# Moving w_down in 4-KB pieces and shifting two zero fills behind the first block's w_down stores

## The chip, the cores, the metric

One core of one Trainium2 chip. The metric is device time in microseconds (us), the median of several executions. All runs quoted here were in the fast state. "Ratio" is the mean time of one kernel's fast runs over that of the other's in the same rounds, so not quite the ratio of the medians that stand beside it. Profile times are counted from the start of the span, which is some 2 us shorter than the measured time.

## The reference

Forward and backward pass of one adaLN-conditioned block: attention of one query token over the last 4096 cached positions, then a gated feed-forward part. Every gradient is an output, so those of the K and V caches are written in full (65,536 positions, zeros outside the window). Only the feed-forward part is touched:

```python
g = jnp.einsum('bsd,df->bsf', x, w_gate)        # D = 1024, F = 3584
u = jnp.einsum('bsd,df->bsf', x, w_up)
h = _sigmoid(g) * u
return jnp.einsum('bsf,fd->bsd', h, w_down)     # w_down is [3584, 1024] bf16
```

## The kernel before

The program moves 248 MB, about half of it zeros (126 MB; "fills", 1 MB each, read from a tile of zeros and issued by GpSimd between other transfers, so that the DMA engines never idle). The feed-forward part runs in 7 blocks of 512 columns. Each block loads w_up and w_gate (GpSimd) and w_down in two halves of 512 KB (SyncE), computes, overwrites the weights in place with their gradients, and stores these (GpSimd). The w_down tile has one buffer, so a block's load waits until the block before has stored the same half.

```python
Z_FOLD = (3, 4)                         # fills at two places ahead of block 0
...
wd_v = ar(152, 8).rearrange("p (i d) -> p i d", i=4)

def wd_dram(t, q, s):                   # half s of block q: rows p and p + 128 on partition p
    return t[q * FB + s * 256:q * FB + s * 256 + 256, :].rearrange("(j p) d -> p j d", p=P)

def load_wd(q, s):
    nc.sync.dma_start(out=wd_v[:, 2 * s:2 * s + 2, :], in_=wd_dram(B_w_down, q, s))

def store_wd(q, s):
    nc.gpsimd.dma_start(out=wd_dram(out_8, q, s), in_=wd_v[:, 2 * s:2 * s + 2, :])
...
load_ug(1, 0, 4); load_ug(1, 4, 4)      # (on two lines in the kernel)
zero(Z_FOLD[1])                         # 4 fills, in GpSimd's order ahead of block 0's stores
...
front(0); gates(0); hh_ops(0)
ffn_mm(0, 0); wd_ttr(0, 0); wd_outer(0, 0)   # wd_outer: VectorE product, then store_wd
ffn_mm(0, 1); wd_ttr(0, 1); dug_part(0); wd_outer(0, 1)
load_wd(1, 0); load_wd(1, 1)
for q in range(NB):
    ...                                 # 8 x (VectorE reduce, ScalarE product), stores of block q
    front(q + 1); gates(q + 1); side(); hh_ops(q + 1)
    ffn_mm(q + 1, 0); wd_ttr(q + 1, 0)
    if q + 2 < NB: load_ug(q + 2, 0, 4)
    wd_outer(q + 1, 0)                  # GpSimd, in order, waits here for VectorE
    ...
```

## Time and profile before

| | before |
|---|---|
| time, median of the first 3 runs | 607.25 us |
| bytes moved, mean rate | 248.19 MB, 410 GB/s |
| 2048-byte packets on the hardware queue | 7680, of which 3584 are w_down loads |

The DMA engines are the bound: they are busy for nine tenths or more of every slice of the span but the first and the last, and no compute engine is. So two numbers matter: how much engine time a byte costs, and how long the engines have too little to move. The prediction shows the lines.

### The profile page before, as it was taken

How to read it: one execution, taken by the hardware profiler on the slowest of the kernel's cores; microseconds unless marked ns; L12 is line 12 of the kernel's file. 1: busy time of each engine (PE TensorE's matmuls, PEld its weight loads, DVE VectorE, ACT ScalarE, POOL GpSimd, SP SyncE). 2: the span in 40 equal slices, each digit the busy share in tenths (PEclk: the TensorE clock that was granted, in tenths of full speed). 3: DMA queues.
4: the chain of work that ended last, by engine and by line, in shares of the span. 5: the costliest groups of instructions: out<-in, count | busy, mean ns of one | idle time of the engine just before them, and what ended most of it. 6: DMA issues, size and time to landing. Idle time of an engine off the chain costs nothing.

```text
span 605.6 us, 10906 instructions
## 1 busy us (share of the span) xinstructions
PE 388.1 (64%) x4496; PEld 265.6 (44%) x4516; DVE 325.1 (54%) x616; ACT 282.4 (47%) x426; POOL 177.8 (29%) x281
## 2 busy tenths in 40 slices
PE   3997788999899989989450454344343277757200
PEld 3995434334344446648340353333333256656200
DVE  3754498999511010060462866756667288778420
ACT  3489514557211014228181768558385833764100
POOL 0002121221322212313342464364542523132230
PEclk9999699999999989989755555555555585755555
DMA  8999999999999999999999999999999999999997
GB/s 353 419 417 421 409 426 413 413 419 420 420 425 426 424 426 419 402 425 411 403 412 391 374 396 409 407 416 404 409 414 420 420 423 411 421 424 425 426 416 282
DMA packets 49522, 248.19 MB, mean 410 GB/s; under 512 B 5629, under 2 KB 5629, under 8 KB 29056
## 3 DMA queue, kind: packets, MB, share of 16 engines
q0 software_dynamic: 37792, 210.78, 90.4%
q1 hardware_dynamic: 11632, 36.71, 17.6%
q8 instruction: 35, 0.57, 0.4%
q14 instruction: 15, 0.12, 0.1%
q10 hardware_dynamic: 48, 0.01, 0.0%
HBM read 61.87 MB, written 185.60 MB: 409 GB/s over the span
## 4 chain that ended last, share of the span: by engine, by line
PE 35%; DMA 29%; DVE 17%; ACT 8%; issue 7%; POOL 1%; ACTq 0%; POOLq 0%; another core or an unknown queue 0%; DVEq 0%; SPq 0%
DMA out_dram<-arena 15%; PE b_ps L687 14%; DMA arena<-in_B_w_down_dram 9%; PE n_ps L635 6%; DVE arena L206 4%; DVE arena L193 4%; DMA arena<-in_B_w_gate_dram 3%; DVE arena L210 3%; DVE junk L210 3%; ACT arena L241 2%; PE t_ps L597 2%; DMA arena<-in_B_w_up_dram 2%; PE tp_wq L453 2%; PE w_ps L394 2%; PE tp_k L434 1%
## 5 line engine op out<-in xcount | busy, mean ns | idle before, releaser
L169 POOL DMA_DIRECT2D out_dram<-zeros x112 | 61.6, 550 | 203.8 <-PE q_ps L471 50.4
L687 PE MATMUL b_ps<-arena 128*128 128x512 bf16 x372 | 88.2, 389 | 0.6
L836 PE MATMUL tp_side<-ident_bf,arena 128*128 128x128 bf16 x416 | 50.1, 297 | 50.9 <-ACT arena L837 41.9
L837 ACT COPY arena<-tp_side 128x1024 bf16<-128x1024 bf16 x52 | 52.1, 1010 | 56.6 <-PE tp_side L836 56.4
L193 DVE TENSOR_TENSOR arena<-arena 128x2048 bf16<-128x2048 bf16 x64 | 76.5, 1224 | 2.3 <-PE n_ps L635 0.3
L210 DVE CUSTOM_DVE_ANT_0 arena<-arena,scr 128x1024 bf16<-128x1024 bf16 x56 | 65.2, 1222 | 9.4 <-ACT scr L969 9.4
L635 PE MATMUL n_ps<-arena 128*128 128x512 bf16 x248 | 65.0, 378 | 7.0 <-DVE arena L193 5.1
L836 PEld LDWEIGHTS <-arena 128*128 128x128 bf16 x416 | 41.1, 137 | 56.2 <-issue 56.1
L241 ACT ACTIVATE arena<-scr,h 128x1024 bf16<-128x1024 bf16 x56 | 61.0, 1145 | 0.0
L687 PEld LDWEIGHTS <-arena 128*128 128x128 bf16 x384 | 37.7, 100 | 46.5 <-issue 7.1
L210 DVE CUSTOM_DVE_ANT_0 junk<-arena,b1k 128x1024 bf16<-128x1024 bf16 x28 | 34.3, 1224 | 26.9 <-DMA arena<-in_B_w_down_dram 26.4
L873 POOL DMA_DIRECT2D out_dram<-arena x42 | 30.7, 734 | 45.8 <-ACT arena L241 38.1
L635 PEld LDWEIGHTS <-arena 128*128 128x128 bf16 x256 | 24.6, 97 | 41.8 <-issue 16.4
L1134 ACT ACTIVATE arena<-ps_kv 128x512 bf16<-128x512 f32 x48 | 26.2, 687 | 28.4 <-PE ps_kv L1130 28.2
L599 ACT CAST arena<-t_ps 128x512 bf16<-128x512 f32 x56 | 30.1, 589 | 12.1 <-PE t_ps L597 12.1
L1130 PE MATMUL ps_kv<-junk,arena 8*128 8x128 bf16 x256 | 26.9, 303 | 11.6 <-DVE arena L206 10.3
L949 PE MATMUL fg<-hh_bf,arena 128*128 128x1 bf16 x224 | 8.1, 166 | 40.5 <-DMA arena<-in_B_w_down_dram 38.8
L1130 PEld LDWEIGHTS <-arena 8*128 8x128 bf16 x256 | 25.0, 140 | 13.3 <-issue 13.3
L202 DVE CAST arena<-b_ps 128x512 bf16<-128x512 f32 x5 | 3.5, 692 | 47.1 <-PE b_ps L687 47.1
L949 PEld LDWEIGHTS <-arena 128*128 128x128 bf16 x224 | 7.1, 105 | 43.5 <-DMA arena<-in_B_w_down_dram 41.4
L455 ACT COPY arena<-tp_wq 128x1024 bf16<-128x1024 bf16 x23 | 21.8, 1032 | 8.1 <-PE tp_wq L453 8.1
L206 DVE TENSOR_SCALAR arena<-arena,cs_col 128x4096 bf16<-128x4096 bf16 (+1 forms) x16 | 16.0, 1017 | 8.2 <-DMA out_dram<-arena 8.0
(297 smaller groups left out, 650.7 us busy)
## 6 DMA issues: line engine op xcount, KB each, us to landing
out_dram<-zeros POOLq DMA_DIRECT2D x112, 1024.0 KB, 13.8
out_dram<-arena POOLq DMA_DIRECT2D x32, 1024.0 KB, 18.9
out_dram<-arena POOLq DMA_DIRECT2D x36, 512.0 KB, 9.3
arena<-in_A_wq_dram SPq DMA_DIRECT2D x8, 1024.0 KB, 19.9
out_dram<-zeros POOLq DMA_DIRECT2D x8, 960.0 KB, 12.7
arena<-in_B_w_down_dram SPq DMA_DIRECT2D x14, 512.0 KB, 10.6
out_dram<-arena POOLq DMA_DIRECT2D x28, 256.0 KB, 10.3
arena<-in_A_wo_dram SPq DMA_DIRECT2D x6, 1024.0 KB, 25.0
```

The source lines that it names most:

```text
L169: ins = nc.gpsimd.dma_start(out=region.bitcast(FP32), in_=zeros[:, :])
L193: return nc.vector.tensor_tensor(out=out, in0=a, in1=b, op=op)
L206: return nc.vector.tensor_scalar(out=out, in0=a, scalar1=s1, scalar2=None, op0=op0)
L210: return nc.vector.tensor_tensor_reduce(out=out, in0=w, in1=b, scale=1.0, scalar=0.0, op0=ALU.mult, op1=ALU.add, accum_out=acc)
L241: return nc.scalar.activation(out=out, in_=b, func=ACT.Copy, scale=col)
L599: nc.scalar.copy(out=o, in_=ps)
L635: mm = nc.tensor.matmul(nbank[k][:, :], lhsT=k_nat[:, g, t_ * DH:(t_ + 1) * DH], rhs=vp[:, t_ % 2, 4 * k:4 * k + 4, :].rearrange("p h d -> ...
L687: mm = nc.tensor.matmul(bbank[p][k][:, :], lhsT=a4[:, p, h, :], rhs=wo_t[u][:, a, k * 512:(k + 1) * 512], start=(i == 0 and a == 0), stop= ...
L836: nc.tensor.transpose(tp[:, i * P:(i + 1) * P], blk[:, i * P:(i + 1) * P], ident_bf[:, :])
L837: nc.scalar.copy(out=blk, in_=tp[:, :])
L873: nc.gpsimd.dma_start(out=ug_part(view, q, j0, n), in_=ug_tile(q, k, j0, n))
L1130: nc.tensor.matmul(ps[:, t4 * DH:(t4 + 1) * DH], lhsT=rows[32 * g:32 * g + HG, t_ * P:(t_ + 1) * P], rhs=hd[32 * g:32 * g + HG, :], start= ...
```

## The change

The intent: larger pieces (two neighbouring rows of 2 KB each on one partition are 4 KB of consecutive memory) and an earlier reload of w_down. As a partition now holds rows 2p and 2p+1, the weights of the gate matmuls are taken with a step of 2, and ScalarE's copy of the gradients' row restores the order.

```diff
-Z_FOLD = (3, 4)
+Z_FOLD = (3, 2, 2)
@@ wd_dram
-        return t[q * FB + s * 256:q * FB + s * 256 + 256, :].rearrange("(j p) d -> p j d", p=P)
+        return t[q * FB + s * 256:q * FB + s * 256 + 256, :].rearrange("(p j) d -> p j d", j=2)
@@ front
+                f0 = 256 * (i // 2) + i % 2
-                    ... lhsT=ug_v[:, q % 2, j // 4, j % 4, k, i * P:(i + 1) * P],
+                    ... lhsT=ug_v[:, q % 2, j // 4, j % 4, k, f0:f0 + 255:2],
@@ dug_part
-        nc.scalar.copy(out=dug_b, in_=tp[:, :])
+        nc.scalar.copy(out=dug_b.rearrange("p (s f j) -> p s f j", s=4, j=2),
+                       in_=tp.rearrange("p (s j f) -> p s f j", s=4, j=2))
@@ after block 0's stores
     wd_outer(0, 1)
+    zero(Z_FOLD[2])
     load_wd(1, 0)
```

## The prediction

> **What bounds the kernel now.** I read the head of the page and its slices first, then the page's chain of waits, then rates by stretch, then the chain in order of time, then GpSimd's own timeline.
>
> ```profile
> span 605.6 us, 10906 instructions
> ...
> DMA  8999999999999999999999999999999999999997
> ...
> DMA packets 49522, 248.19 MB, mean 410 GB/s; under 512 B 5629, under 2 KB 5629, under 8 KB 29056
> ...
> PE 35%; DMA 29%; DVE 17%; ACT 8%; issue 7%; POOL 1%; ACTq 0%; POOLq 0%; another core or an unknown queue 0%; DVEq 0%; SPq 0%
> ```
>
> The DMA engines are at 9 or more tenths in every slice but the first and the last, while no compute engine is (PE 64%, DVE 54%). 248.19 MB at 410 GB/s is 605 us: the span. The chain names PE first, but chain shares only say who was waited for; the bytes set the end. So this change, which moves the same bytes, can gain in two ways only: a better rate while bytes flow, or less time in which they don't. The stage it touches is the feed-forward part, about 280 to 480 us.
>
> ```profile
> 320.00:330.00 10.00, 0.14 (x5) 0.14 (x6) 0.16 (x1) 0.00 (x0) 2.29 (x4) 0.50 1.09 410
> 330.00:335.00 5.00, 2.67 (x48) 2.26 (x46) 4.43 (x9) 1.01 (x1) 1.57 (x3) 0.50 0.67 251
> 335.00:340.00 5.00, 2.17 (x18) 1.72 (x17) 3.61 (x10) 2.40 (x3) 3.65 (x6) 0.50 1.06 398
> 340.00:350.00 10.00, 4.33 (x79) 4.00 (x79) 7.88 (x14) 9.95 (x11) 3.27 (x6) 0.50 1.07 394
> ```
>
> The columns are the stretch, its length, busy time of PE, PEld, DVE, ACT and POOL with instructions, then the TensorE clock, the DMA share and GB/s. There is one hole: 251 GB/s at 330 to 335 us. The next stretches come back to 390 to 420, and nowhere later until the tail does the DMA share fall under 1.
>
> ```profile
> 306.13 13.08 DMA out_dram<-arena
> 319.21 0.02 SPq L856
> 319.24 0.04 issue
> 319.27 10.54 DMA arena<-in_B_w_down_dram
> 329.82 0.02 issue
> 329.84 1.22 DVE junk L210
> ...
> 333.43 0.71 POOL out_dram L859
> ```
>
> This is the chain (start, length, what) through the hole. The store of block 0's first w_down half takes 13.08 us to land, because it queues behind what GpSimd issued before. Only then may the load of block 1's half go into the same buffer; it takes 10.54 us. VectorE then works, and GpSimd can issue the next store at 333.43.
>
> ```profile
> 304.42 0.56 POOL L169 DMA_DIRECT2D out_dram<-zeros  x1 [0.58 <-DMA arena<-in_B_w_up_dram]
> 306.13 0.72 POOL L859 DMA_DIRECT2D out_dram<-arena  x1 [1.15 <-DMA arena<-in_B_w_gate_dram]
> 307.50 0.73 POOL L859 DMA_DIRECT2D out_dram<-arena  x1 [0.64 <-ACT arena L837]
> 312.52 1.51 POOL L873 DMA_DIRECT2D out_dram<-arena  x2 [4.30 <-ACT arena L241]
> ...
> 323.63 0.76 POOL L869 DMA_DIRECT2D arena<-in_B_w_gate_dram  x1 [0.55 <-DMA out_dram<-arena]
> 333.43 0.71 POOL L859 DMA_DIRECT2D out_dram<-arena  x1 [9.04 <-DVE arena L206]
> ```
>
> GpSimd issues in order. From 324.4 to 333.4 us it stands still for 9.04 us waiting for that product, and what it queued before runs dry at about 333: the hole. It also stands idle 4.30 us before 312.52, right after the two stores.
>
> **What the Trainium skill says.** (1) "DMA: Bandwidth & Descriptors", Why small descriptors are slow (HBM only): each packet has a fixed cost of some 3 cycles inside the engine. The trace agrees and gives the size. In its packet records (each packet's queue, bytes and time), SyncE's 2048-byte packets take 84 ns where little else interferes (505 to 545 us on the records' own clock, which runs some 7 us ahead of the span's), 4096-byte ones 159 ns and 8192-byte ones 309 ns: 9 ns plus 75 ns per 2 KB. (2) The same page, Queues, rings and completion order: an engine switches between queue rows at packets. That fits 2048-byte packets that took 126 ns while the other queue was full. (3) "SBUF — State Buffer", Door 1: The DMA port swizzle, in its note on cachelines: bf16 reads may step up to 8 elements free, while PSUM has 8-byte ones. The new weight loads step by 2 in SBUF, the new ScalarE copy reads PSUM 128 elements apart. No strided instance of either is in this trace. (4) "TensorE: Matmul & The Clock Gate", Weight-path perf modes: the fast load reads columns packed or strided. Here only packed ones show, 104 ns each.
>
> **The change part by part.**
>
> *w_down loads.* 14 loads of 512 KB are 3584 packets of 2048 bytes, 1792 of 4096 after. Each pair saves 2 x 84 - 159 = 9 ns: 1792 x 9 / 16 engines = **1.0 us**. As a check I fitted the engine time of all 5-us stretches outside the hole to packet counts: 86.0 (plus or minus 1.8) ns for a 2-KB packet, 160.9 for a 4-KB one of the same queue, so 11 ns a pair and 1.2 us. The DMA engines are full here, so this counts whole.
>
> *w_down stores.* No 2048-byte packet is in the software queue; the rows already go two to a packet. The w_o gradient's stores, also with 2-KB rows, take 159 to 160 ns a packet, as the 4-KB-row stores at the end do. So the store gains about **0 us**, 0.2 at most (2 ns x 1792 / 16).
>
> *The two fills.* The stores' data were ready before they were issued: VectorE ended the first product at 300.2 us and the second at 303.7, but four fills stood ahead of the stores in GpSimd's order. With two of them behind, the first store goes out at about 303.0 (the slot of the third fill) and has 2 x 1.05 MB less ahead of it, 2.1 MB / 0.42 = 5.0 us. It lands at about 314.2 in place of 319.2, the load at 324.8 in place of 329.8, and GpSimd resumes at about 328.4. The bytes queued ahead are the same sum, so they still last to about 333 us: the new work arrives some 4.6 us before the queue is dry and the hole closes. The fills themselves go into GpSimd's 4.30-us gap and hold up nothing. Gain: (410 - 251) x 5 / 410 = 1.94 us, plus (410 - 398) x 5 / 410 = 0.15 us: **2.1 us**. I leave out 340 to 350 us, since 394 is near what the stage has with its 1-KB rows.
>
> *Strided weights and the permuted copy.* Fronts: 448 weight loads and matmuls, 64 a block, about 1.9 us a block; with a step of 2 elements I expect no change. The copy of the gradients' row (1012 ns, 7 times) may be slower by its step of 256 bytes in PSUM; I take 0 to 0.5 us each. It stands on the chain in several blocks, but GpSimd still waits there for DMA landings (0.2 to 2 us before many issues), so the queue is full and little of it reaches the end: **0 us**, at worst 7 x 0.5 = 3.5.
>
> Sum: 1.0 + 0 + 2.1 = 3.1 us from 607.25, or 604.15. I say 604.2.
>
> **Rivals.** (a) *The hole moves.* The buffer chain (load, VectorE, store, load) stays, and the hole could open one block later: closing one gap only lets GpSimd arrive early at the next in-order wait. For it: every block has one such wait, 2 to 2.5 us on the later stores. Against: in the later blocks the queue never ran dry (DMA share 1.06 and more). If it holds, the fills bring 0 to 1 us: 605.2 to 606.3.
> (b) *Permutation costs.* The strided weight load doubles (1.9 us a block, in front of the gates) or the copy does (1 us). For: PSUM's small lines. Against: TensorE and ScalarE are half idle here, and the DMA backlog (10.6 us from issue to landing for a w_down load, by the median) covers them. If all of it showed, 7 x 2.9 = 20 us, 624; I give this a few per cent, and a tenth of it (606) more.
> (c) *No merging*: the load keeps 2-KB packets because the two rows are described one by one. Then only the fills gain: 605.2.
> (d) *More than the sum*: the load of two rows lands sooner in every block and opens slack elsewhere, as the stage runs at 404 to 411 GB/s where fills alone run at 425. If a quarter of that difference in 190 us came back, 1.7 us more: 602.5.
>
> **Range and chances.** All likely branches lie between 602.4 (d) and 606.3 (a), which I take as the range. A gain of 2% needs 595.1 us, four times my sum, with no source for it in the profile; a loss of 2% needs 619.4, the worst of (b). Chances: faster 0.01, same 0.98, slower 0.01.
>
> **What would show it.** Hardware-queue packets of 2048 bytes fall by 3584 and those of 4096 bytes rise by 1792, at 159 ns; the software queue's count stays. The stretch at 330 to 335 us has over 400 GB/s and a DMA share over 1; the first w_down load of block 1 goes out at about 314 us; GpSimd's wait before its next store (9.04 us) starts and ends some 5 us earlier. The weight loads of the fronts stay near 104 ns and the copy near 1012 ns. A new stretch under 380 GB/s after 340 us would mean rival (a); a longer copy or weight load with gaps in the DMA share, (b); unchanged packet counts, (c).

## The result, and the profile after

604.05 us (median of 6 runs, 603.54 to 604.98) against 607.29 of the kernel before: ratio 0.995, interval 0.9937 to 0.9963. The forecast was 604.2. By the 2% measure this is "same".

First the hardware queue of both kernels, which carries SyncE's transfers, as the software queue carries GpSimd's (queue, packets, MB, share of engine time). Before:

```profile
q1 hardware_dynamic: 11632, 36.71, 17.6%
```

After, with the page's totals:

```profile
span 602.8 us, 10936 instructions
...
DMA packets 47730, 248.19 MB, mean 412 GB/s; under 512 B 5629, under 2 KB 5629, under 8 KB 27264
...
q1 hardware_dynamic: 9840, 36.71, 18.0%
```

1792 packets fewer for the same bytes: the two rows are moved as one. By the packet records of the trace, those of 2048 bytes went from 7680 to 4096, those of 4096 bytes from 1024 to 2816, and the software queue kept 37,792. The *share* of the queue rose all the same, but not by the load's data: between 250 and 480 us the records of 2048 and 4096 bytes took 378 us before and 321 after (all engines added up), while 240 records of 4 bytes went from 61 to 140 us. So the share isn't a measure of the load's cost.

Rates by stretch after (the same columns as in the prediction; DMA share and GB/s are the last two):

```profile
330.00:335.00 5.00, 2.51 (x21) 2.19 (x22) 3.62 (x10) 2.55 (x4) 2.70 (x5) 0.50 1.08 410
335.00:340.00 5.00, 1.56 (x14) 1.24 (x12) 5.00 (x9) 5.00 (x6) 0.79 (x3) 0.50 1.08 418
340.00:350.00 10.00, 5.32 (x104) 4.74 (x103) 5.29 (x13) 7.90 (x10) 6.03 (x9) 0.50 1.17 411
325.00:360.00 35.00, 14.64 (x204) 12.57 (x205) 23.91 (x52) 20.67 (x23) 16.78 (x26) 0.50 1.13 413
360.00:480.00 120.00, 47.69 (x669) 41.02 (x668) 74.20 (x160) 80.58 (x88) 54.71 (x83) 0.50 1.12 414
```

And before, the two wide ones, which the prediction didn't have:

```profile
325.00:360.00 35.00, 14.58 (x216) 12.64 (x217) 23.05 (x48) 18.83 (x21) 15.79 (x23) 0.50 1.02 380
360.00:480.00 120.00, 47.69 (x674) 40.87 (x674) 76.99 (x163) 78.34 (x86) 56.91 (x84) 0.50 1.10 412
```

The hole is gone: 251 has become 410. Over the whole disturbed stretch the rate rose from 380 to 413 GB/s, which is (413 - 380) x 35 / 413 = 2.8 us. In the steady blocks after it, it rose from 412 to 414, 120 x 2 / 414 = 0.6 us. The two together are 3.4 us; the span fell by 2.8 in these two profiles and the medians by 3.2.

GpSimd's timeline after (start, length, what, idle before it and what ended that):

```profile
302.88 0.57 POOL L859 DMA_DIRECT2D out_dram<-arena  x1 [2.16 <-DMA out_dram<-zeros]
304.66 0.56 POOL L859 DMA_DIRECT2D out_dram<-arena  x1 [1.20 <-DVE arena L206]
305.30 0.53 POOL L169 DMA_DIRECT2D out_dram<-zeros  x1
306.65 0.53 POOL L169 DMA_DIRECT2D out_dram<-zeros  x1 [0.82 <-DMA arena<-in_B_w_up_dram]
312.88 1.52 POOL L873 DMA_DIRECT2D out_dram<-arena  x2 [5.70 <-ACT arena L241]
...
324.76 0.75 POOL L869 DMA_DIRECT2D arena<-in_B_w_gate_dram  x1 [2.20 <-DMA out_dram<-zeros]
328.21 0.56 POOL L859 DMA_DIRECT2D out_dram<-arena  x1 [2.69 <-issue]
```

The first store goes out at 302.88 (forecast 303.0), the two fills lie in the gap ahead of 312.88, and block 1's first store goes out at 328.21 (forecast 328.4, before 333.43). The 9.04-us stand has become 2.69. It no longer ends with VectorE, though; VectorE's product for that store was ready at 326.62:

```profile
325.74 0.88 DVE L206 TENSOR_SCALAR arena<-b1k,hh 128x1024 bf16<-128x1024 bf16 x2
```

Before, the store followed 0.29 us after the product; here it took 1.59 us (1.46 in e9, the same kernel again). "Issue" means that the profile shows nothing that GpSimd waited for, so what held it is open.

### The profile page after: what moved, and what is told of

Same layout as the page of the kernel before. It is cut to its first block, busy times and chain, and to the rows that moved or that the text cites. A ratio compares the mean times of both kernels' runs of the same rounds, so it can differ in the third digit from the quotient of the medians.

```text
span 602.8 us, 10936 instructions
## 1 busy us (share of the span) xinstructions
PE 389.8 (65%) x4516; PEld 265.6 (44%) x4516; DVE 324.8 (54%) x616; ACT 282.8 (47%) x426; POOL 174.2 (29%) x281
## 4 chain that ended last, share of the span: by engine, by line
DMA 35%; PE 34%; DVE 14%; issue 7%; ACT 5%; POOL 2%; ACTq 0%; POOLq 0%; DVEq 0%; SPq 0%
DMA out_dram<-arena 17%; PE b_ps L687 14%; DMA out_dram<-zeros 8%; DMA arena<-in_B_w_down_dram 7%; PE n_ps L635 6%; DVE arena L210 4%; DVE arena L193 4%; PE t_ps L597 2%; DMA arena<-in_B_w_up_dram 2%; DVE arena L206 2%; DVE junk L210 2%; ACT arena L241 2%; PE tp_wq L453 2%; PE w_ps L394 1%; PE tp_k L434 1%
## 5 line engine op out<-in xcount | busy, mean ns | idle before, releaser
L687 PE MATMUL b_ps<-arena 128*128 128x512 bf16 x384 | 89.5, 389 | 0.0
L836 PEld LDWEIGHTS <-arena 128*128 128x128 bf16 x416 | 41.2, 137 | 59.2 <-issue 59.1
L687 PEld LDWEIGHTS <-arena 128*128 128x128 bf16 x384 | 37.7, 100 | 46.4 <-issue 7.1
L635 PEld LDWEIGHTS <-arena 128*128 128x128 bf16 x256 | 24.6, 97 | 41.8 <-issue 16.4
L933 PE MATMUL fg<-h_bf,arena 128*128 128x1 bf16 x448 | 15.6, 166 | 19.0 <-DMA arena<-in_B_w_up_dram 12.4
L933 PEld LDWEIGHTS <-arena 128*128 128x128 bf16 x448 | 14.4, 105 | 20.2 <-DMA arena<-in_B_w_up_dram 13.0
## 6 DMA issues: line engine op xcount, KB each, us to landing
out_dram<-zeros POOLq DMA_DIRECT2D x8, 960.0 KB, 13.1
```

The lines of the kernel that those rows point to most:

```text
L635: mm = nc.tensor.matmul(nbank[k][:, :], lhsT=k_nat[:, g, t_ * DH:(t_ + 1) * DH], rhs=vp[:, t_ % 2, 4 * k:4 * k + 4, :].rearrange("p h d -> ...
L687: mm = nc.tensor.matmul(bbank[p][k][:, :], lhsT=a4[:, p, h, :], rhs=wo_t[u][:, a, k * 512:(k + 1) * 512], start=(i == 0 and a == 0), stop= ...
L836: nc.tensor.transpose(tp[:, i * P:(i + 1) * P], blk[:, i * P:(i + 1) * P], ident_bf[:, :])
L933: nc.tensor.matmul(gu[:, col + i:col + i + 1], lhsT=ug_v[:, q % 2, j // 4, j % 4, k, f0:f0 + 255:2], rhs=h2_bf[:, j:j + 1], start=(j == 0) ...
```

## The experiments

Ten kernels. Those of one group ran on one chip beside the same runs of the kernel before: its median was 607.38 us in the first group (e1 to e4), 607.06 in the second (e5, e6, e8, e9) and 607.18 in the third (e7, e10). My theory at this point: two independent gains, 9 ns for each pair of load packets and a hole of 2.1 us. The rivals: one part does it all, or the parts work through the same thing.

### e1: the pieces without the fills

```diff
-Z_FOLD = (3, 2, 2)
+Z_FOLD = (3, 4, 0)      # in the changed kernel
```

> The changed kernel with all four fills put back ahead of block 0's w_down stores; the 4-KB pieces, the stepped weight loads and the permuted copy stay. My theory (two separate gains, 9 ns per pair of load packets and a hole of some 2 us): the hole at 330 to 335 us is back (under 300 GB/s) and the time is 1.0 us under the kernel before, about 606.2. Rival 1 (the gain is all the fills'): 607.2. Rival 2 (the 4-KB pieces bring most of it, by landing sooner and stores being cheaper to issue): 604.5 or less, with the hole gone or much smaller.

605.22 us (5 runs), ratio 0.9965 (0.9952 to 0.9977): 2.2 us under the kernel before, twice what I had given the pieces (for how much of it is theirs, see below). The stretches:

```profile
330.00:335.00 5.00, 2.13 (x31) 1.88 (x32) 3.73 (x9) 1.01 (x1) 2.55 (x4) 0.50 1.06 404
335.00:340.00 5.00, 2.38 (x20) 1.89 (x18) 3.64 (x7) 3.45 (x4) 2.53 (x4) 0.50 1.07 385
...
325.00:360.00 35.00, 15.59 (x224) 13.48 (x225) 24.64 (x52) 19.58 (x22) 15.75 (x24) 0.50 1.13 402
```

The hole did *not* come back: 404 and 385, and 402 over the wide stretch. Rival 2 of the expectation has this hole right, if not the time. TensorE's timeline shows when block 1's w_down is there, by the start of the first matmuls on it. Before:

```profile
329.86 0.59 PE L949 MATMUL fg<-hh_bf,arena 128*128 128x1 bf16 x16 [12.08 <-DMA arena<-in_B_w_down_dram]
```

Pieces only:

```profile
327.10 0.58 PE L950 MATMUL fg<-hh_bf,arena 128*128 128x1 bf16 x16 [8.80 <-DMA arena<-in_B_w_down_dram]
```

The load went out at 319.27 us before and at 319.02 here, nearly the same time, but its data were used 2.8 us earlier, and so GpSimd got on at 330.67 in place of 333.43. That isn't all the work of larger packets. e8 (below) has the steps and the permuted copy as here, but the 2-KB packets and all transfers of the kernel before:

```profile
327.84 0.58 PE L950 MATMUL fg<-hh_bf,arena 128*128 128x1 bf16 x16 [9.65 <-DMA arena<-in_B_w_down_dram]
```

There the load went out at 318.96, and GpSimd got on at 331.41. e8 differs from e1 only in the rows of w_down's loads and stores, so it is the closer comparison: against it the pieces bring the first half 0.7 us earlier and the second 1.2 us (331.60 in place of 332.82), and 402 in place of 387 GB/s over the wide stretch. In time e1 is 1.6 us faster than e8 by the ratios (0.7 to 2.6 by the two intervals; two chips). That the pieces bring more than the 1.0 us of packet cost is therefore likely by the stretch, but not shown by the time. Whether the steps or mere scatter moved the load in e8 isn't shown.

### e2: the fills without the pieces

```diff
-Z_FOLD = (3, 4)
+Z_FOLD = (3, 2, 2)      # in the kernel before
     wd_outer(0, 1)
+    zero(Z_FOLD[2])
```

> The kernel before with only the two fills moved behind block 0's w_down stores; 2-KB packets stay. My theory: first load of block 1 goes out near 314 us, the hole closes, and the time falls by 2.1 us to about 605.1. Rival 1 (fills alone): 604.1. Rival 2 (the hole moves to a later block as long as packets are small): 606.5 to 607.2, with a stretch under 380 GB/s after 340 us.

605.68 us (8 runs), ratio 0.9971 (0.9961 to 0.9982): 1.7 us. The hole is filled (397 GB/s at 330 to 335, 403 at 335 to 340, 408 over the wide stretch). The load went out at 314.26, 5.0 us earlier as forecast, but was used at 326.86, only 3.0 us earlier: it took 12.6 us in place of 10.6. My step, that it takes 10.54 us at any time, was wrong here too. The packet records show what came between: while the first half's packets moved, the software queue moved 2.1 MB, against 1.4 MB before. Why more came between, the runs don't show.

Alone the parts give 2.2 and 1.7 us, 3.9 together; the change gives 3.1 to 3.2. The intervals of these times are too wide to show an overlap. The stretch shows it: over 325 to 360 us the pieces raise the rate by 22 GB/s (15 against e8) and the fills by 28, together more than the 33 of the whole change. Both close the same hole.

### e3: 2-KB load packets in the changed kernel

```diff
-        nc.sync.dma_start(out=wd_v[:, 2 * s:2 * s + 2, :], in_=wd_dram(B_w_down, q, s))
+        for j in range(2):
+            nc.sync.dma_start(out=wd_v[:, 2 * s + j, :], in_=wd_dram(B_w_down, q, s)[:, j, :])
```

> The changed kernel, but each 512-KB w_down load goes as two loads of 256 KB, one per row of the pair, so the hardware queue carries 2048-byte packets again (3584 more, 1792 of 4096 fewer); the stores stay in 4-KB pieces and the fills stay moved. If the 9 ns per pair of load packets is what the pieces bring: 1.0 us slower than the changed kernel, about 605.0. If it is the stores that gain (cheaper to issue on GpSimd, 558 in place of 722 ns, or faster in the engine): no slower than 604.2. Twice as many load instructions could add a little latency; that would show as a longer time from issue to landing, not as more engine time.

604.70 us (5 runs), ratio 0.9962 (0.995 to 0.9975), against 0.9951 of the changed kernel beside other runs (e9): 0.7 us slower, with 411 GB/s in the wide stretch, so no hole to speak of. This is near the 1.0 us of packet cost, but the intervals overlap: by the time alone it isn't shown. (e3 also has twice the load instructions.) What the packet records do show is the cost of each: 84 ns for 2 KB, 159 for 4 KB.

### e4: 1-KB load packets in the kernel before

```diff
-        nc.sync.dma_start(out=wd_v[:, 2 * s:2 * s + 2, :], in_=wd_dram(B_w_down, q, s))
+        for c in (slice(0, 512), slice(512, 1024)):
+            nc.sync.dma_start(out=wd_v[:, 2 * s:2 * s + 2, c], in_=wd_dram(B_w_down, q, s)[:, :, c])
```

> The kernel before with each w_down load cut in two by columns, so its packets are 1024 bytes: 7168 of them in place of 3584. This raises the suspected cost instead of removing it. By 9 ns plus 36.6 ns per KB a packet takes 46 ns: (7168 x 46 - 3584 x 84) / 16 engines = 1.8 us more, about 609.1. If a packet's fixed cost is hidden behind the other queue's packets, no change: 607.3. If the hole grows because the load lands later, more than 610, with under 250 GB/s at 330 to 335 us.

611.66 us (5 runs), ratio 1.0072 (1.0059 to 1.0084): 4.3 us slower, not 1.8. The packets cost what was forecast (46 ns each by the records). The rest is the hole, which grew: 277 GB/s at 330 to 335 us and 198 at 335 to 340, and 357 over the wide stretch, (380 - 357) x 35 / 413 = 1.9 us more than before. 1.8 + 1.9 = 3.7 of the 4.3 us.

### e5: the hole filled in another way

One fill is taken from the first group after the feed-forward part and put just ahead of GpSimd's stand. Nothing lands earlier; the queue is longer when GpSimd stops.

```diff
-Z_END = (2, 1, 1, 0, 0)
+Z_END = (1, 1, 1, 0, 0)      # in the kernel before
                 load_ug(q + 2, 0, 4)
+            if q == 0:
+                zero(1)
             wd_outer(q + 1, 0)
```

> The kernel before, with one fill (1 MB) taken from the first group after the feed-forward stage and put into GpSimd's order just ahead of its 9-us stand before block 1's first w_down store. Nothing lands earlier, the packets stay at 2 KB; only the queue holds 1 MB more when GpSimd stops. Theory (the hole costs what the DMA engines don't move in it, 2.1 us or 0.86 MB): the hole nearly closes (over 380 GB/s at 330 to 335 us) and the time is 605.3. Rival (the time comes from the earlier landing of the w_down store and load, not from the idle DMA): no gain, 607.4, or a loss as the store lands later. If the fill is missed at its old place, a hole opens near 480 us and the gain is lost: 607.4 with that hole seen.

606.03 us (21 runs), ratio 0.9982 (0.9976 to 0.9989): 1.0 us, half of what I expected, but clearly more than nothing. The hole closed in part:

```profile
330.00:335.00 5.00, 2.30 (x32) 1.77 (x30) 4.53 (x9) 1.43 (x2) 2.05 (x4) 0.50 0.98 363
...
325.00:360.00 35.00, 14.68 (x218) 12.73 (x219) 23.40 (x49) 19.26 (x21) 16.33 (x24) 0.50 1.08 402
```

So time does come from the DMA engines having work, without any earlier landing: GpSimd's store went out at 332.95, only 0.5 us sooner than before, and its issues run 0.5 us early from 300 us on, ahead of the edit. The rival "it is the earlier landing as such" would have had no gain.

### e6: one fill in place of two

```diff
-Z_FOLD = (3, 2, 2)
+Z_FOLD = (3, 3, 1)      # in the changed kernel
```

> The changed kernel with one fill behind the stores in place of two. The 4-KB pieces alone left 1.0 us of the hole (385 to 404 GB/s at 330 to 345 us). Theory (the two parts overlap: the pieces let the load land 2.5 us sooner and already close most of the hole): one fill is enough, 604.2, as with two. Rival (each fill adds its own share): 604.7, half way between the pieces alone (605.2) and the change (604.05).

603.98 us (5 runs), ratio 0.9952 (0.9939 to 0.9964), the same as with two (0.9951). With the 4-KB pieces, one fill seems enough; but the rival's 604.7 lies inside the interval, so it isn't excluded. The profiled run still has one weak stretch (352 GB/s at 340 to 345 us).

### e8: the steps and the permuted copy alone

The edit is the "front" and "dug_part" hunks of the diff in the kernel before. As the transfers stay as they were, the results are wrong on purpose (relative error over 1).

> The kernel before with the stepped weight loads and the permuted copy of the gradients' row, and nothing else: transfers stay as they were, so the results for the feed-forward part are wrong on purpose. Theory: free, weight loads 104 ns, copy 1012 ns, time 607.4. Rival (they cost something that the rest of the change pays for): over 608.

606.58 us (13 runs), ratio 0.9992 (0.9984 to 1.0). Weight loads 104 ns by the median, the copy 1012 ns, both as before. The steps cost nothing. If anything this kernel is 0.5 us faster, at the edge of the interval, and its profile has a smaller hole (387 GB/s over the wide stretch against 380) although the transfers are the same; e1 has to be read against it.

### e9: the changed kernel again

> The changed kernel as it is, to have it beside these runs on the same chip. 604.05 expected, ratio 0.9947; if the pieces alone (605.2) and the fills alone (605.7) had added up it would be 603.5.

603.93 us (5 runs), ratio 0.9951 (0.9939 to 0.9964). The median doesn't reach the 603.5 of a plain sum, but the interval includes it.

### e7 and e10: the ends of both dials

e7 puts all four fills behind the stores, `Z_FOLD = (3, 0, 4)` in the changed kernel:

> The changed kernel with all four fills of that group behind the stores. The first store's data are ready at 300.2 us, so it can go out at most 2.7 us earlier than in the change. Theory (with the hole closed there is nothing left to gain): 604.0. Rival (an earlier store still helps): under 603.5. If GpSimd now stands still at 296 to 300 us with too little queued: a stretch under 380 GB/s near 305 us and over 604.5.

604.25 us (6 runs), ratio 0.9948 (0.9935 to 0.996): no more to gain. It gives a little away at 300 to 310 us (366 and 368 GB/s): the weak stretch that the expectation allowed for came, but not its loss of time.

e10 is the changed kernel with the edit of e4, so 1-KB load packets with the fills moved:

> The changed kernel with its w_down loads cut in two by columns: 7168 packets of 1024 bytes in place of 1792 of 4096, fills moved, stores in 4-KB pieces. Engine time: (7168 x 46 - 1792 x 159) / 16 = 2.8 us more than the changed kernel. Theory (a packet's 9 ns plus a hole that comes back only if the load lands late): 606.8 with the queue still full at 330 to 335 us. If the load lands so late that the hole opens in spite of the fills, more: 608 and a stretch under 330 GB/s. If small packets cost nothing by themselves and the 1-KB loads with the fills unmoved (4.3 us slower than the kernel before) lost it all in the hole: 604 to 605.

610.64 us (5 runs), ratio 1.0053 (1.004 to 1.0065): 6.2 us over the changed kernel by the ratios and 6.7 by the medians, not 2.8. The hole opened in spite of the fills:

```profile
340.00:350.00 10.00, 3.04 (x24) 2.55 (x24) 8.91 (x16) 8.86 (x9) 3.99 (x6) 0.50 0.93 313
325.00:360.00 35.00, 13.86 (x208) 11.91 (x208) 21.45 (x43) 18.25 (x20) 13.11 (x20) 0.50 1.02 367
```

The load went out at 314.31 us, as in the change, but its first half was all there only at 329.19, and its second at 336.19. Here is block 1's w_down load in nine of the kernels. The last column is taken from the packet records: what the software queue moved from the start of the first half's first packet to the end of its last.

| kernel | packets | fills | went out | first half all used by TensorE | second half | software queue meanwhile |
|---|---|---|---|---|---|---|
| e1, pieces only | 4 KB | ahead | 319.02 | 327.10 (8.1 us) | 331.60 | 0.9 MB |
| e8, steps only | 2 KB | ahead | 318.96 | 327.84 (8.9 us) | 332.82 | 1.1 MB |
| e5, backlog | 2 KB | ahead | 318.81 | 329.38 (10.6 us) | 333.08 | 1.4 MB |
| before | 2 KB | ahead | 319.27 | 329.86 (10.6 us) | 333.65 | 1.4 MB |
| e4 | 1 KB | ahead | 319.65 | 332.70 (13.1 us) | 336.33 | 2.0 MB |
| the change | 4 KB | moved | 313.93 | 323.35 (9.4 us) | 327.50 | 1.4 MB |
| e3, two loads a half | 2 KB | moved | 314.33 | 325.47 (11.1 us) | 329.59 | 1.6 MB |
| e2, fills only | 2 KB | moved | 314.26 | 326.86 (12.6 us) | 330.24 | 2.1 MB |
| e10 | 1 KB | moved | 314.31 | 329.19 (14.9 us) | 336.19 | 3.0 MB |

With the fills in one place, the smaller the load's packets, the more of the software queue comes between them and the later the load is through. So packet size bears on the landing, and so does the company: with 2-KB packets it is anything from 8.9 to 12.6 us. Over all 14 loads the median from issue to landing is 10.6 us in the four kernels that load whole halves in 2-KB packets (before, e2, e5, e8) and 9.3 to 10.4 us in the five with 4-KB ones (the change, e1, e6, e7, e9).

This fits what the Trainium skill says in "DMA: Bandwidth & Descriptors", Queues, rings and completion order: an engine takes turns between queues packet by packet. The software queue's records are of 4 or 8 KB; a queue with smaller packets would move fewer bytes per turn. But a packet of that page can hold several descriptors (single pieces of memory), and whether a record of the trace is one of its packets, the runs don't show. From 4 to 1 KB the second half comes 8.7 us later. e10 and e4 also need twice the load instructions (0.54 us each on SyncE in e10), so not all of their delay need be turns.

### One sum for all of them

Take 604.0 us for the changed kernel without a hole. Add the shortfall in the stretch from 325 to 360 us, (413 - rate) x 35 / 413, and the engine time of the load packets by the records, over that of 4-KB ones: 1.0 us for 2 KB and 2.8 for 1 KB.

| kernel | GB/s, 325 to 360 | shortfall | packets | sum | measured |
|---|---|---|---|---|---|
| before | 380 | 2.8 | 1.0 | 607.8 | 607.3 |
| e1, pieces only | 402 | 0.9 | 0 | 604.9 | 605.2 |
| e2, fills only | 408 | 0.4 | 1.0 | 605.4 | 605.7 |
| e3, 2-KB loads | 411 | 0.2 | 1.0 | 605.2 | 604.7 |
| e4, 1-KB loads | 357 | 4.7 | 2.8 | 611.5 | 611.7 |
| e5, backlog | 402 | 0.9 | 1.0 | 605.9 | 606.0 |
| e6, one fill | 405 | 0.7 | 0 | 604.7 | 604.0 |
| e7, four fills | 413 | 0 | 0 | 604.0 | 604.3 |
| e8, steps only | 387 | 2.2 | 1.0 | 607.2 | 606.6 |
| e10, 1-KB loads, fills | 367 | 3.9 | 2.8 | 610.7 | 610.6 |

All ten agree to 0.7 us, which is about what one profile may differ from the median run (e8 and before have the same transfers, and 387 and 380 GB/s). No wait of an engine is in this sum. It is bookkeeping, though, and no proof of a cause: all kernels move nearly the same bytes, so a stretch with a lower rate must show in the time. And the packet cost of the loads inside the stretch (3 of 14, an estimate) counts in both columns, 0.2 us for 2 KB and 0.6 for 1 KB.

## Why the prediction was right

**The bound and the total** were right: bytes over rate, 604.2 forecast, 604.05 measured.

**The packet cost** was right where it can be seen: 84, 159 and (e4, e10) 46 ns, 9 ns of each independent of its size. That "the trace agrees" with the skill's 3 cycles (the prediction's point 1) holds only for there being a fixed cost: 75 ns for the 64 pieces of 32 bytes in 2 KB, which that section takes to be one cycle each, make a cycle 1.17 ns, so that 9 ns are some 8 cycles (an estimate). The records' clock runs 10.7 us ahead of the span's, not 7; the 84 ns are the same in either stretch. In the steady blocks from 360 to 480 us, the kernels with 1-KB loads have 409 GB/s, those with 2-KB ones 412 to 413 and those with 4-KB ones 414 to 415. That stretch has about 8 of the 14 loads, so 1.0 x 8 / 14 = 0.6 us was due there between 2 and 4 KB, and 2 / 413 x 120 = 0.6 us is what shows.

**The hole** was the right mechanism, and moving the fills closes it (e2). The first store and GpSimd's resumption in the changed kernel were met to within 0.2 us, the resumption by luck. Three steps of the working were wrong:

- "the load at 324.8 in place of 329.8" took the landing time of 10.54 us as fixed. It is 8.1 to 14.9 us in the table above and depends on the packets and the company. In the change it was 9.4 us. With 2-KB packets (e2) it was 12.6, and GpSimd went on at 330.43, not at 328.4.
- "and GpSimd resumes at about 328.4" took the load and VectorE's product to be what GpSimd waits for. In the change the load was used at 323.35, 1.5 us earlier than forecast, and the product was ready at 326.62; GpSimd went on at 328.21 after a wait that the profile puts down to nothing. The two errors cancel.
- "I leave out 340 to 350 us, since 394 is near what the stage has". It isn't: the changed kernel has 411 there. The disturbance lasted to 360 us and was worth 2.8 us, not 2.1.

**The sum of independent terms** (1.0 + 0 + 2.1) is the step that failed while its total held. The pieces with their steps alone bring 2.2 us (1.6 against the steps without the pieces, e8), and the rate shows them closing part of the hole, from 380 or 387 to 402 GB/s; the fills alone bring 1.7; both 3.1 to 3.2. That an underrated hole and an unforeseen overlap roughly cancel is luck.

**The rivals**: (a), the hole moves to a later block, is refuted (no stretch of 5 us under 400 GB/s from 340 us to the tail at 595 us in the change). (b), the steps cost something, is refuted by e8. (c), no merging, by the packet counts. (d), quicker landing: it is there in every block (median 9.7 us in place of 10.6), but the rate of the steady blocks rose by no more than the packet cost, so what it is worth lies in the one hole.

**GpSimd's stand** was forecast to keep its length and move 5 us earlier. It ended 5.2 us earlier but began 1.1 us later (325.51 in place of 324.39), so it shrank to 2.69 us. GpSimd's issues before it didn't move with the store: they go out within 0.6 us of their old times, but for the last, which waited 2.20 us for a fill to land.

No version was found that beats the changed kernel; one, two or four fills behind the stores lie within 0.3 us.

## What to carry to other kernels

Where the DMA engines are the bound, look for the stretch in which the rate falls and ask which in-order issue was late; here three edits that brought work there in time (fills, pieces, backlog) each raised the rate, and fills and pieces together raised it by less than their sum. A packet's size counts twice: by its fixed cost (1.0 us here between 2 and 4 KB, 1.8 between 1 and 2 KB), and by how soon a load gets through beside a full queue of larger packets, which matters if the next issue waits for that load. Before two edits are added up, run each against a twin that has all the rest: e1 against the kernel before gave 2.2 us, against e8 1.6. Price a transfer's landing time from runs with the same packets and the same company, not as a constant.

## What the Trainium skill lacked or had wrong

- "DMA: Bandwidth & Descriptors", Why small descriptors are slow (HBM only): it gives a fixed cost of about 3 cycles a packet beside one cycle for 32 bytes. The records show 46, 84, 159 and 309 ns for 1, 2, 4 and 8 KB, thus 9 ns fixed, some 8 such cycles (an estimate from 75 ns for 2 KB).
- The same page, Queues, rings and completion order: the turns by packet are described, but not what follows for a load: with 1, 2 and 4-KB packets and the fills moved, the first half of the w_down load took 14.9, 11.1 to 12.6 and 9.4 us, with 3.0, 1.6 to 2.1 and 1.4 MB of the other queue between its packets.
- The same page, Anatomy of one DMA — SWDGE (gpsimd) path: it calls descriptor generation small and variable. GpSimd's issue of a 512-KB w_down store took 722 ns with 2-KB rows and 558 ns with 4-KB ones (medians of 14).
- "SBUF — State Buffer", Door 1: The DMA port swizzle: it warns of non-contiguous PSUM access for matmuls and says nothing of ScalarE. A ScalarE copy that reads PSUM in steps of 256 bytes took 1012 ns, the same as in order (e8).
